# A state-space and SwiGLU block on one core: token blocks of two tiles, and down's weights split once

## The chip, the cores and the metric

The kernel runs on one core of a Trainium2 chip. The core has TensorE for matrix products (PE in the profile, with its weight loads as PEld), VectorE (DVE), ScalarE (ACT) and GpSimd (POOL) for elementwise work, and SyncE (SP), which here issues every DMA. The metric is the device time of one execution in microseconds.

## The reference

The input has 2048 tokens of 448 features. Two residual branches follow each other; both are modulated by six vectors drawn from a condition c.

```
mod = (silu(c) @ w_mod) -> sa, ca, ga, sb, cb, gb
h = layernorm(x) * (1 + ca) + sa
x = x + ga * (causal_conv(h, K) + h * Dskip)      # K from A, B, C, dt, 256 states per feature
h = layernorm(x) * (1 + cb) + sb
x = x + gb * ((silu(h @ w_gate) * (h @ w_up)) @ w_down)   # w_gate, w_up 448 x 1792, w_down 1792 x 448
```

The convolution's kernel K(l) is a sum of exponentials. When its exponents are small over all 2048 steps, the kernel takes K as K(0) plus a slope times l; the convolution is then running sums along the tokens. A test on the chip picks this path (the small path, the one that these inputs take) or a general one.

## The kernel before

The 2048 tokens are 16 tiles of 128 rows; F = 1792 is 14 slices of 128. Tiles are grouped in blocks of 2, 2, 3, 3, 3 and 3 (`BLOCKS`). A block runs the feed-forward branch for its tiles (`ffn`): for each slice f, `gate_up(f)` forms gate and up for all tokens of the block, one matmul of 256 or 384 columns for each pair of weight part and input part, and `down(f - 1)` accumulates the former slice's result for each tile in a PSUM bank (`dn0` to `dn2`). I call gate_up(f) with down(f - 1) a step.

Matmuls use the fast float32r type. To keep float32's precision each operand is split in a high part, rounded by a ScalarE copy, and a low part, the difference; three products of parts replace one. Inputs are split in `transposes` (hhi, hlo), the product silu(gate) * up in `gate_up` (phi, plo, lines 664 to 668), gate's and up's weights in `split_w` (lines 90 to 95), and down's in `split_d` (wdh on ScalarE, line 634; wdl on GpSimd, line 635). Gate's and up's parts are kept on chip after the first block; down's unsplit slices are kept (`wdn`), and split again in every block. In the last block down's weights are first multiplied by gb, on GpSimd.

The first block is special (`fresh`): weights arrive during it. SyncE loads three slices ahead into three staging buffers (`stage`), one slice being four DMAs for gate and up (lines 78 and 79) and one for down (line 84); a staging buffer is free once its slice is split. Before the first block a preamble computes the modulation, K and the first two tiles.

While a block runs, the first branch of the next block's tiles is computed between its steps: `n1` statistics, h (s0), two products with the gates (s1), adding the running sums and splitting (s2), the skip term (s3), three triangular matmuls into `cv` and a bank (s4), and passing the last row on as running sums through a small DMA, line 798 (s5); then `n2` statistics, the normalised tile (`make_xn`), and four groups of transposes between gate_up(13) and down(12), which I call the transition.

The order on every engine is the program's order (`manual_schedule`). The table `TIMES` sets it by hand: its numbers are half steps of a block, h // 2 being the slice after which a stage is put and h % 2 whether before or after down. Tiles in PSUM come from a rotating pool of four banks (`bank`), two for each slice, one for a scan, four for a transition; a bank is given out again when all readers of its former use are done.

```
at(f, late): after gate_up(f), before (late = 0) or after (late = 1) down(f - 1)
at(NF - 1, 0, transposes, nx, new_fl)
```

Of the kernel before, what the change touches and what calls it, by code (L numbers as in the profile page):

```python
# [21 lines left out]
NS = 3  # L22
BLOCKS = [2, 2, 3, 3, 3, 3]
# [3 lines left out]

TIMES = (
# [15 lines left out]
def tile_kernel(ctx, tc, x, a_re, a_im, b_re, b_im, c_re, c_im, log_dt, dskip,  # L44
# [25 lines left out]
    wgu, raw, wdn = {}, {}, {}  # L70
    stage = [const.tile([128, 2, 4, 128], F32, name=f"raw{q}") for q in range(NS)]

# [9 lines left out]
    def load_d(pool, j):  # L82
        wdn[j] = pool.tile([128, D], F32, name=f"wd{j}")
        sy.dma_start(wdn[j], wd[j * 128:(j + 1) * 128, :])

# [13 lines left out]
    tok = const.tile([128, 1], F32)  # L99
    run = const.tile([128, 2, D], F32)  # L100
    ca1 = const.tile([128, D], F32)
# [20 lines left out]
    class Norm:  # L122
# [10 lines left out]
        def root(self, ts):  # L133
            rs = small.tile([128, MB], F32, name="rs" + self.tag)
            n = len(ts)
            po.tensor_scalar(rs[:, 0:n], self.mv[:, 0:n, 1], EPS, None, op0=OP.add)
            po.tensor_tensor(rs[:, 0:n], rs[:, 0:n], mhalf.to_broadcast([128, n]), op=OP.pow)
            for q, i in enumerate(ts):
                self.of[i] = self.mv[:, q, 0:1], rs[:, q:q + 1]
# [8 lines left out]
    def make_h(h, i, part=None):  # L148
        m, rs = n1.of[i]
# [8 lines left out]
    def make_xn(i, new, src=None):  # L158
        src = xs[i] if src is None else src
        xn[i] = new()  # L160
        for o, a, n in ((0, 0, D), (D, 384, 64)):
            ve.tensor_scalar(xn[i][:, o:o + n], src[:, a:a + n], *n2.of[i], op0=OP.subtract, op1=OP.mult)

    def transposes(ts, new):
        n = len(ts) * 128
        for k in range(4):
# [3 lines left out]
            fl = new()  # L170
            sc.activation(hhi[:, k, 0:n], ps[:, 0:n], AF.Identity, scale=cb1c[:, k:k + 1], bias=sbc[:, k:k + 1])
            if k % 2:
                sc.activation(fl[:, 0:n], ps[:, 0:n], AF.Identity, scale=cb1c[:, k:k + 1], bias=sbc[:, k:k + 1])
# [64 lines left out]
    with tc.tile_pool(name="pre", bufs=1) as pre, tc.tile_pool(name="wm", bufs=6) as wm:  # L238
# [166 lines left out]
        for q in range(2):  # L405
            make_xn(q, lambda: pre.tile([128, 512], F32, name="xn", bufs=2), os[q])
# [9 lines left out]
        transposes(TILES[0], lambda: pre.tile([128, MB * 128], F32, name="fl", bufs=2))  # L416
# [6 lines left out]
        for z in range(2):  # L423
            sc.copy(run[0:1, z, :], o[32 * z:32 * z + 1])
# [194 lines left out]
    def run_blocks(pools, st, first=None):  # L619
        work, hid = pools.work, pools.hid  # L620
        new_xn = lambda: work.tile([128, 512], F32, name="xn", bufs=MB)
        new_fl = lambda: hid.tile([128, MB * 128], F32, name="p")
        def ffn(ts, fresh, last, todo):
            n = len(ts) * 128
            dn = [psd.tile([128, 512], F32, name=f"dn{q}") for q in range(len(ts))]
            pp, wp = {}, {}
            qz = [(q, z) for z in range(3) for q in range(len(ts))]

            def split_d(j):
                if last:  # L630
                    po.tensor_tensor(wdn[j], wdn[j], gb, op=OP.mult)
                hi = hid.tile([128, D], F32R, name="wdh")
                lo = hid.tile([128, D], F32R, name="wdl")
                sc.copy(hi, wdn[j])  # L634
                po.tensor_tensor(lo, wdn[j], f32(hi), op=OP.subtract)  # L635
                wp[j] = hi, lo

            def gate_up(f, nw):
                head = fresh and f == 0
                if not head:  # L640
                    split_d(f)
# [22 lines left out]
                ve.tensor_tensor(p[:, 0:n], p[:, 0:n], ps[1][:, 0:n], op=OP.mult)  # L664
                if nw is not None and not head:
                    split_w(nw, 1)
                sc.copy(hi[:, 0:n], p[:, 0:n])  # L667
                ve.tensor_tensor(lo[:, 0:n], p[:, 0:n], f32(hi[:, 0:n]), op=OP.subtract)  # L668
# [30 lines left out]
            for q, i in enumerate(ts):  # L699
                t = dn[q][:, 0:D]  # L700
                if not last:
                    t = new_xn()[:, 0:D]
                    ve.tensor_tensor(t, dn[q][:, 0:D], gb, op=OP.mult)
                ve.tensor_tensor(xs[i], xs[i], t, op=OP.add)
                sy.dma_start(out[i * 128:(i + 1) * 128, :], xs[i])
# [3 lines left out]
        if first is not None:  # L709
# [8 lines left out]
            transposes(TILES[0], new_fl)  # L718
        for b, ts in enumerate(TILES):
            todo = {}  # L720
            if b + 1 < len(TILES):
# [8 lines left out]
                root1, *times, root2, shift = TIMES[min(b, 2)]  # L730
# [4 lines left out]
                for q, (i, hs) in enumerate(zip(nx, times)):  # L735
# [3 lines left out]
                    go(h, n2.stat, i, nx)  # L739
# [4 lines left out]
                at(NF - 1, 0, transposes, nx, new_fl)  # L744
# [4 lines left out]
    def small_path(pools):  # L749
# [3 lines left out]
        def s0(i):  # L753
            h = work.tile([128, D], F32, name="h")
# [5 lines left out]
        def s1(i):  # L760
            h = vs[i]
            v0 = work.tile([128, D], F32, name="v0")
            v1 = work.tile([128, D], F32R, name="v1")
            po.tensor_tensor(v0, h, gm0, op=OP.mult)  # L764
            po.tensor_tensor(v1, h, gm1, op=OP.mult)  # L765
            vs[i] = h, v0, v1

        def s2(i):
            h, v0, v1 = vs[i]
            ve.tensor_tensor(v0[0:1], v0[0:1], run[0:1, 0, :], op=OP.add)  # L770
            po.tensor_tensor(v1[0:1], f32(v1[0:1]), run[0:1, 1, :], op=OP.add)  # L771
# [6 lines left out]
        def s3(i):  # L778
            h = vs[i][0]
            po.tensor_tensor(h, h, gd, op=OP.mult)  # L780
# [10 lines left out]

        def s5(i):
            o, s = vs.pop(i)
            if i + 1 < NT:
                e = slice(96, 128)
                sc.copy(run[e, 1, :], s[e])
# [88 lines left out]
```

## Time and profile before

| | |
|---|---|
| three runs | 515.14, 515.95, 516.49 us, median 515.95 |
| profiled execution | 516.8 us |
| its span, first to last instruction | 514.9 us, mean granted clock 0.982 |
| TensorE busy | 486.1 us, 94%, 2747 matmuls |
| weight loads busy | 454.5 us, 88% |
| VectorE, ScalarE, GpSimd busy | 305.1, 189.0, 226.3 us |
| chain that ended last | TensorE 78%, VectorE 10%, DMA 3% |
| DMA | 26.07 MB, 21.80 MB of them read from HBM |

All times in the views below are microseconds from the start of the span, unless marked ns. A row of the chain or of a timeline has start, duration, engine (SPq is SyncE's queue of DMA issues), source line, operation, destination <- sources, and a count where equal rows are merged; a bracket gives idle time before it and what ended that. A row of the groups has busy time, mean ns of one, and idle time before. Matmuls overlap in the engine's pipeline, so the time of one is read from the start of the next.

The blocks begin at 49.7, 118.4, 180.8, 263.7, 346.6 and 429.5 us, as told by their first gate matmuls; the preamble is what lies ahead of 49.7.

### The profile page before, as it was taken

The numbers are of one execution on the slowest core, as the hardware profiler recorded it, in microseconds if no ns is written. First come the engines' busy times: TensorE is split into PE (matmuls) and PEld (weight loads), VectorE is DVE, ScalarE is ACT, GpSimd is POOL, SyncE is SP. The second block draws the span as 40 slices with busy tenths as digits, with TensorE's granted clock in tenths as the row PEclk, the third lists the DMA queues.
The fourth block names the chain that finished last, engine by engine and source line by source line (L and its number), as shares of the span: only waits on it lengthen the run. The fifth ranks groups of instructions, "written<-read, shape, count | busy, mean of one in ns | idle before, by whom it ended". The sixth has DMA issues, their size and how long they took to land.

```text
span 514.9 us, 7291 instructions
## 1 busy us (share of the span) xinstructions
PE 486.1 (94%) x2747; PEld 454.5 (88%) x2747; DVE 305.1 (59%) x509; ACT 189.0 (37%) x388; POOL 226.3 (44%) x209
## 2 busy tenths in 40 slices
PE   6679979799989999999999999999999999999995
PEld 4345969689879999999999999999999999999995
DVE  1898889987687762675373477275377447211222
ACT  4247735544323432333242333242233324222231
POOL 1468453641765325483212555312446423344330
PEclk8988998999999999999999999999999999999999
DMA  7996555402000020000021000003000001000001
GB/s 209 259 222 174 150 153 158 136 28 90 0 2 2 0 91 0 2 2 0 1 71 37 1 2 1 2 2 107 1 0 2 0 1 53 1 1 0 2 0 61
DMA packets 25860, 26.07 MB, mean 51 GB/s; under 512 B 2232, under 2 KB 25144, under 8 KB 25816
## 3 DMA queue, kind: packets, MB, share of 16 engines
q1 hardware_dynamic: 25816, 25.52, 17.8%
q8 instruction: 23, 0.38, 0.3%
q14 instruction: 21, 0.17, 0.1%
HBM read 21.80 MB, written 3.67 MB: 49 GB/s over the span
## 4 chain that ended last, share of the span: by engine, by line
PE 78%; DVE 10%; DMA 3%; issue 3%; ACT 3%; SPq 2%; POOL 0%; POOLq 0%; DVEq 0%; ACTq 0%
PE bank L653 49%; PE dn L679 23%; PE bank L187 1%; PE bank L169 1%; DVE gu L95 1%; DMA dsk<-in_A_Dskip_dram 1%; DMA raw<-in_B_w_up_dram 1%; DVE scr L334 1%; DVE v L770 1%; DVE h L151 1%; DMA wd<-in_B_w_down_dram 1%; DVE plo L668 1%; SPq L78 1%; DVE t L342 1%; PE cv L786 1%
## 5 line engine op out<-in xcount | busy, mean ns | idle before, releaser
L653 PE MATMUL bank<-hhi,gu 128*128 128x384 f32 (+1 forms) x1169 | 213.4, 322 | 0.4 <-DVE gu L93 0.4
L653 PEld LDWEIGHTS bank<-hhi,gu 128*128 128x128 f32 x1169 | 193.1, 190 | 3.6 <-DVE gu L93 0.6
L635 POOL TENSOR_TENSOR wdl<-wd,wdh 128x448 fp32r<-128x448 f32 x84 | 102.2, 1219 | 203.3 <-ACT wdh L634 191.1
L653 PE MATMUL bank<-hlo,gu 128*128 128x384 f32 (+1 forms) x668 | 132.6, 321 | 0.0
L664 DVE TENSOR_TENSOR p<-p,bank 128x384 f32<-128x384 f32 (+1 forms) x84 | 42.5, 506 | 131.2 <-PE bank L653 127.0
L653 PEld LDWEIGHTS bank<-hlo,gu 128*128 128x128 f32 x668 | 111.0, 190 | 0.0
L667 ACT CAST phi<-p 128x384 fp32r<-128x384 f32 (+1 forms) x84 | 40.1, 477 | 151.0 <-DVE p L664 151.0
L668 DVE TENSOR_TENSOR plo<-p,phi 128x384 fp32r<-128x384 f32 (+1 forms) x84 | 53.8, 641 | 41.0 <-ACT phi L667 41.0
L659 ACT ACTIVATE p<-bank 128x384 f32<-128x384 f32 (+1 forms) x83 | 37.8, 456 | 68.8 <-PE bank L653 68.8
L679 PE MATMUL dn<-wdh,plo 128*128 128x448 f32 x224 | 59.9, 368 | 2.8 <-DVE plo L668 2.6
L679 PE MATMUL dn<-wdh,phi 128*128 128x448 f32 x224 | 60.2, 369 | 1.2 <-ACT phi L667 1.2
L679 PE MATMUL dn<-wdl,phi 128*128 128x448 f32 x224 | 59.5, 366 | 0.8 <-POOL wdl L635 0.8
L634 ACT CAST wdh<-wd 128x448 fp32r<-128x448 f32 x84 | 47.6, 567 | 31.7 <-PE dn L679 31.6
L679 PEld LDWEIGHTS dn<-wdh,plo 128*128 128x128 f32 x224 | 41.8, 188 | 7.5 <-DVE plo L668 4.3
L679 PEld LDWEIGHTS dn<-wdl,phi 128*128 128x128 f32 x224 | 42.0, 188 | 4.6 <-POOL wdl L635 1.1
L679 PEld LDWEIGHTS dn<-wdh,phi 128*128 128x128 f32 x224 | 39.8, 188 | 3.1 <-ACT phi L667 1.6
L764 POOL TENSOR_TENSOR v<-h,gm 128x448 f32<-128x448 f32 x14 | 16.2, 1154 | 14.2 <-DVE h L153 14.2
L774 ACT CAST vh<-v 128x448 fp32r<-128x448 f32 x14 | 7.9, 566 | 33.1 <-DVE v L770 33.1
L187 PE MATMUL bank<-wmt,cs 112*128 112x448 f32 (+1 forms) x32 | 15.4, 632 | 4.8 <-DMA wmt<-in_w_mod_dram 4.8
L765 POOL TENSOR_TENSOR v<-h,g 128x448 fp32r<-128x448 f32 x14 | 18.5, 1319 | 0.0
L771 POOL TENSOR_TENSOR v<-v,run 1x448 fp32r<-1x448 f32 x14 | 17.0, 1212 | 2.5 <-DMA run<-run 1.5
L187 PEld LDWEIGHTS bank<-wmt,cs 112*128 112x128 f32 (+1 forms) x32 | 6.2, 205 | 12.6 <-issue 9.6
(167 smaller groups left out, 447.1 us busy)
## 6 DMA issues: line engine op xcount, KB each, us to landing
wmt<-in_w_mod_dram SPq DMA_DIRECT2D x6, 784.0 KB
x<-in_A_u_dram SPq DMA_DIRECT2D x16, 224.0 KB
out_dram<-x SPq DMA_DIRECT2D x16, 224.0 KB
wd<-in_B_w_down_dram SPq DMA_DIRECT2D x14, 224.0 KB
raw<-in_B_w_gate_dram SPq DMA_DIRECT2D x14, 192.0 KB
raw<-in_B_w_up_dram SPq DMA_DIRECT2D x14, 192.0 KB
raw<-in_B_w_gate_dram SPq DMA_DIRECT2D x14, 64.0 KB
raw<-in_B_w_up_dram SPq DMA_DIRECT2D x14, 64.0 KB
```

The source lines that it names most:

```text
L187: pe.matmul(ps[0:rows, 0:D], cs[:, k:k + 1].to_broadcast([P, rows]), w[k], start=k == 0, stop=k == 3)
L634: sc.copy(hi, wdn[j])
L635: po.tensor_tensor(lo, wdn[j], f32(hi), op=OP.subtract)
L653: pe.matmul(ps[s][:, 0:n], w[:, s, a], (hlo if lo else hhi)[:, k, 0:n], start=not lo and a == 0, stop=lo and k == 3)
L659: sc.activation(p[:, 0:n], ps[0][:, 0:n], AF.Silu)
L664: ve.tensor_tensor(p[:, 0:n], p[:, 0:n], ps[1][:, 0:n], op=OP.mult)
L667: sc.copy(hi[:, 0:n], p[:, 0:n])
L668: ve.tensor_tensor(lo[:, 0:n], p[:, 0:n], f32(hi[:, 0:n]), op=OP.subtract)
L679: pe.matmul(dn[q][:, 0:D], u[:, cs], v, start=f == 0 and z == 0, stop=f == NF - 1 and z == 2)
L764: po.tensor_tensor(v0, h, gm0, op=OP.mult)
L765: po.tensor_tensor(v1, h, gm1, op=OP.mult)
L771: po.tensor_tensor(v1[0:1], f32(v1[0:1]), run[0:1, 1, :], op=OP.add)
```

## The change

- Blocks are eight of two tiles. The x tiles on chip are four instead of six, as are other buffers that go by the block's size, and `TIMES` has new half steps.
- Down's slices arrive in three staging buffers of their own (`stage_d`). Their parts are made once, in the first block, and kept for all blocks; the low part is made by VectorE. SyncE loads down's slice f + 3 behind gate's and up's slice f + 5, where before both parts of slice f + 5 came together.
- In the first block, the branch of the next tiles takes the products with the gates and the skip term on VectorE, and the triangular matmuls of the first product in full float32, with the running sums added by one-row matmuls (s14); nothing is split there.
- The product silu * up and the transposed inputs are written back to their PSUM banks instead of SBUF, and split from there.
- `make_xn` runs on ScalarE, with a bias that GpSimd makes (two small operations in `root`), save for the very first tile.
- gb is multiplied on VectorE at the end of every block; the very last tile is finished and stored in two halves.

```diff
-BLOCKS = [2, 2, 3, 3, 3, 3]
+BLOCKS = [2] * 8
 TIMES = (
-    (3, (6, 8, 8, 9, 11, 11), (12, 14, 15, 17, 20, 20), 21, (24, 25)),
-    (3, (6, 8, 9, 10, 10, 11), (10, 10, 13, 13, 15, 16), (15, 16, 18, 18, 21, 21), 22, (24, 24, 24)),
-    (3, (7, 8, 8, 10, 10, 10), (10, 13, 13, 14, 14, 15), (14, 17, 17, 18, 18, 19), 20, (24, 24, 24)),
+    (3, (4, 6, 9, 10, 12), (7, 8, 16, 17, 18), 19, (20, 21)),
+    (3, (4, 5, 9, 11, 12, 13, 14), (6, 8, 16, 17, 18, 19, 20), 21, (22, 23)),
 )
...
+    stage_d = [const.tile([128, D], F32, name=f"rawd{q}") for q in range(NS)]
...
     def load_d(pool, j):
-        wdn[j] = pool.tile([128, D], F32, name=f"wd{j}")
+        wdn[j] = stage_d[j % NS]
+        wp[j] = [pool.tile([128, D], F32R, name=f"wd{q}{j}") for q in "hl"]
         sy.dma_start(wdn[j], wd[j * 128:(j + 1) * 128, :])
+
+    def split_d(j):
+        hi, lo = wp[j]
+        sc.copy(hi, wdn[j])
+        ve.tensor_tensor(lo, wdn[j], f32(hi), op=OP.subtract)
...
+            if self is n2:
+                po.tensor_tensor(ng[:, 0:n], self.mv[:, 0:n, 0], rs[:, 0:n], op=OP.mult)
+                po.tensor_scalar(ng[:, 0:n], ng[:, 0:n], -1.0, None, op0=OP.mult)
...
-            ve.tensor_scalar(xn[i][:, o:o + n], src[:, a:a + n], *n2.of[i], op0=OP.subtract, op1=OP.mult)
+            if on_v:
+                ve.tensor_scalar(xn[i][:, o:o + n], src[:, a:a + n], m, rs, op0=OP.subtract, op1=OP.mult)
+            else:
+                sc.activation(xn[i][:, o:o + n], src[:, a:a + n], AF.Identity, scale=rs, bias=ng)
...
-                ve.tensor_scalar(fl[:, 0:n], ps[:, 0:n], cb1c[:, k:k + 1], sbc[:, k:k + 1], op0=OP.mult, op1=OP.add)
-            ve.tensor_tensor(hlo[:, k, 0:n], fl[:, 0:n], f32(hhi[:, k, 0:n]), op=OP.subtract)
+                ve.tensor_scalar(ps[:, 0:n], ps[:, 0:n], cb1c[:, k:k + 1], sbc[:, k:k + 1], op0=OP.mult, op1=OP.add)
+            ve.tensor_tensor(hlo[:, k, 0:n], ps[:, 0:n], f32(hhi[:, k, 0:n]), op=OP.subtract)
...
-            def split_d(j):
-                if last:
-                    po.tensor_tensor(wdn[j], wdn[j], gb, op=OP.mult)
-                hi = hid.tile([128, D], F32R, name="wdh")
-                lo = hid.tile([128, D], F32R, name="wdl")
-                sc.copy(hi, wdn[j])
-                po.tensor_tensor(lo, wdn[j], f32(hi), op=OP.subtract)
-                wp[j] = hi, lo
...
-                if not head:
+                if fresh and not head:
                     split_d(f)
...
-                ve.tensor_tensor(p[:, 0:n], p[:, 0:n], ps[1][:, 0:n], op=OP.mult)
+                ve.tensor_tensor(ps[1][:, 0:n], p[:, 0:n], ps[1][:, 0:n], op=OP.mult)
...
-                sc.copy(hi[:, 0:n], p[:, 0:n])
-                ve.tensor_tensor(lo[:, 0:n], p[:, 0:n], f32(hi[:, 0:n]), op=OP.subtract)
+                sc.copy(hi[:, 0:n], ps[1][:, 0:n])
+                ve.tensor_tensor(lo[:, 0:n], ps[1][:, 0:n], f32(hi[:, 0:n]), op=OP.subtract)
...
-                    pools.load(f + 2 + NS)
+                    pools.load(f + 2 + NS, f + NS)
...
-                t = dn[q][:, 0:D]
-                if not last:
-                    t = new_xn()[:, 0:D]
-                    ve.tensor_tensor(t, dn[q][:, 0:D], gb, op=OP.mult)
-                ve.tensor_tensor(xs[i], xs[i], t, op=OP.add)
-                sy.dma_start(out[i * 128:(i + 1) * 128, :], xs[i])
+                t = new_xn()[:, 0:D]
+
+                h = D // 2 if last and q == len(ts) - 1 else D
+                for a in range(0, D, h):
+                    c_ = slice(a, a + h)
+                    ve.tensor_tensor(t[:, c_], dn[q][:, c_], gb[:, c_], op=OP.mult)
+                    ve.tensor_tensor(xs[i][:, c_], xs[i][:, c_], t[:, c_], op=OP.add)
+                    sy.dma_start(out[i * 128:(i + 1) * 128, c_], xs[i][:, c_])
...
+        def s14(i):
+            h, v0, v1 = vs[i]
+            o = psd.tile([128, 512], F32, name="cv")[:, 0:D]
+            s = bank()[:, 0:D]
+            pe.matmul(o, f32(tri), v0, start=True, stop=False)
+            pe.matmul(s, tri, v1, start=True, stop=False)
+            pe.matmul(s, f32(tri[0:1, :]), run1[0:1], start=False, stop=True)
+            pe.matmul(o, f32(tri[0:1, :]), run0[0:1], start=False, stop=True)
+            s3(i, True)
+            ve.tensor_tensor(xs[i], h, xs[i], op=OP.add)
+            vs[i] = o, s
...
+        return lambda fresh: (s0, lambda i: s1(i, True), s14, s5) if fresh else (s0, s1, s2, s3, s4, s5)
```

More of the change, by code (lines that the diff above doesn't have):

```diff
@@ L415, in tile_kernel @@
             split_w(0, z)
-        transposes(TILES[0], lambda: pre.tile([128, MB * 128], F32, name="fl", bufs=2))
+        transposes(TILES[0])
         o = psd.tile([128, 512], F32, name="cv")[:, 0:D]
@@ L422, in tile_kernel @@
         sc.copy(xs[1], os[1])
-        for z in range(2):
-            sc.copy(run[0:1, z, :], o[32 * z:32 * z + 1])
+        sc.copy(run0[0:1], o[0:1])
+        sc.copy(run1[0:1], o[32:33])
         po.tensor_scalar(hd[0], gm1, tok, None, op0=OP.mult)
@@ L753, in s0, with s1 @@
         def s0(i):
-            h = work.tile([128, D], F32, name="h")
+            h = work.tile([128, D], F32, name="h", bufs=2)
             make_h(h, i)
             vs[i] = h
-        def s1(i):
+        def s1(i, on_v=False):
             h = vs[i]
[L762 to L765, printed above, removed]
+            v0 = work.tile([128, D], F32, name="v0", bufs=2)
+            v1 = work.tile([128, D], F32R, name="v1", bufs=2)
+            for v, g in ((v0, gm0), (v1, gm1)):
+                (ve if on_v else po).tensor_tensor(v, h, g, op=OP.mult)
             vs[i] = h, v0, v1
@@ L795, in s5 @@
                 e = slice(96, 128)
[L796 to L797 removed]
+                sc.copy(run1[e], s[e])
+                ve.scalar_tensor_tensor(run0[e], run1[e], 128.0, o[e], op0=OP.mult, op1=OP.add)
                 sy.dma_start(run[0:1], run[127:128])
```

55 lines of the change are left out of this document (28 added, 27 removed).

## The prediction

> **What bounds the kernel now.** I read the page's busy shares first (TensorE busy 94% of the span), then a table of stages: the first block of two tiles, the second, and the third, the first of three tiles. Columns after the length are busy time and instruction count of TensorE, its weight loads, VectorE, ScalarE and GpSimd, then granted clock, DMA share and GB/s.
>
> ```profile
> 49.70:118.40 68.70, 61.07 (x411) 56.11 (x410) 60.64 (x90) 37.39 (x83) 34.10 (x28) 0.98 0.43 123
> 118.40:180.80 62.40, 60.09 (x416) 56.38 (x415) 47.55 (x80) 24.06 (x55) 32.37 (x30) 0.97 0.06 19
> 180.80:263.70 82.90, 82.90 (x457) 80.84 (x457) 46.51 (x83) 28.83 (x56) 33.70 (x30) 1.00 0.05 15
> ```
>
> The third block has TensorE busy for all of 82.90 us: matmuls alone set it, and 34 us of GpSimd beside it cost nothing. Slack to win lies only in the first two blocks. Next the chain of waits, for the pace of a step (gate and up for one slice of F, then down for the slice before): two tiles in the second block, three in the third.
>
> ```profile
> 124.85 2.61 PE bank L653 x22
> ...
> 128.69 2.62 PE bank L653 x22
> ...
> 188.53 1.82 PE dn L679 x9
> ...
> 194.23 1.82 PE dn L679 x9
> ```
>
> A step takes 3.84 us with two tiles (1.92 a tile) and 5.70 with three (1.90 a tile). In the second block 14 x 3.84 = 53.8, 1.3 of transposes and three scans of 0.6 (three matmuls of 448 columns at 0.203, a twelfth of the 2.44 us of L679 quoted below) make 56.9 of 62.4 us: 5.5 us of stall. In the first block, 14 steps, one transition (1.0), two scans and the small extras make about 57 of 68.7: some 12 us of stall.
>
> Then what the first block waits for: SyncE's DMA issues, the chain at one of them, and ScalarE's split of a weight slice.
>
> ```profile
> 62.68 0.38 SPq L78 DMA_DIRECT2D raw<-in_B_w_gate_dram  x1
> ...
> 87.08 0.64 SPq L798 DMA_DIRECT2D run<-run  x1
> ...
> 90.17 1.66 SPq L84 DMA_DIRECT2D wd<-in_B_w_down_dram  x1
> ```
> ```profile
> 90.17 3.98 DMA wd<-in_B_w_down_dram
> ```
> ```profile
> 66.01 0.41 ACT L91 CAST gu<-raw 128x256 fp32r<-128x256 f32 x1 [0.81 <-DMA raw<-in_B_w_up_dram]
> ```
>
> SyncE issues five sets (gate, up and down of one slice) without a gap in 24.4 us, 4.88 us a set, slower than TensorE's 3.84; ScalarE's wait shows a late landing. A down slice lands 3.98 us after its issue began, 2.3 after it ended. VectorE is the other limit (60.64 of 68.7 busy):
>
> ```profile
> 73.30 1.25 DVE L95 TENSOR_TENSOR gu<-raw,gu 64x256 fp32r<-64x256 f32 x1
> ...
> 102.58 0.42 DVE L664 TENSOR_TENSOR p<-p,bank 128x256 f32<-128x256 f32 x1
> 102.92 0.95 DVE L93 TENSOR_TENSOR gu<-raw,gu 128x768 fp32r<-128x768 f32 x1
> 103.79 0.42 DVE L668 TENSOR_TENSOR plo<-p,phi 128x256 fp32r<-128x256 f32 x1
> 104.24 0.42 DVE L95 TENSOR_TENSOR gu<-raw,gu 64x256 fp32r<-64x256 f32 x1
> 104.69 0.62 DVE L789 TENSOR_TENSOR x<-h,x 128x448 f32<-128x448 f32 x1
> ```
>
> The same operation (L95) takes 0.42 us or 1.25: the long ones stand beside a GpSimd operation on two SBUF tensors.
>
> **The change, part by part.**
>
> *Down's split once.* It removes 70 of the 84 GpSimd subtractions of this row, and as many ScalarE copies (mean 1219 and 567 ns):
>
> ```profile
> L635 POOL TENSOR_TENSOR wdl<-wd,wdh 128x448 fp32r<-128x448 f32 x84 | 102.2, 1219 | 203.3 <-ACT wdh L634 191.1
> ...
> L634 ACT CAST wdh<-wd 128x448 fp32r<-128x448 f32 x84 | 47.6, 567 | 31.7 <-PE dn L679 31.6
> ```
>
> In the later blocks that is worth nothing: TensorE covers it (third stage row). In the first block 14 subtractions move to VectorE, 14 x 0.62 = 8.7 us more there (the price of the 128x448 row L789), and GpSimd falls nearly silent, which takes the long forms away. VectorE's step is then 0.42 + 0.95 + 0.42 + 0.42 + 0.62 = 2.83; the work of two tiles (about a dozen operations of 0.62 each, gates and skip now among them, splits and scan inputs gone) adds some 15. That is 2.83 x 14 + 15, about 55 us: it fits, but steps that carry tile work come to 5.4.
>
> *Loads in the first block.* Down's slices move behind gate and up of a slice two later in SyncE's queue, through three staging tiles, each freed by a split three steps earlier, so those waits are met early. All sets stay needed, so the pace stays 4.88. From 62.68, eight sets (gate and up of 6 to 13, down of 4 to 11) end at 101.7; two moves of the running sums (0.64 each) and two more slices of down (1.66 each) end at 106.3; the last lands 2.3 later, 108.6. Behind it come ScalarE's copy 0.57 and SiLU 0.4 (as a 256-column copy, 0.41 at L667 below), product 0.42, copy 0.41, subtraction 0.42 with gaps of some 0.1 each: 111.2. The fourth pair of transposes (0.26) and two downs (2.44) follow: the second block starts at 113.9 rather than 118.4: -4.5. Bounds: TensorE alone (next item) 111.0, so -7.4; no gain, 0.
>
> *The branch in float32.* These matmuls run two records each:
>
> ```profile
> 14.11 1.67 PE L320 MATMUL dn<-x,ident 128*128 128x448 f32 x4
> ```
>
> Two take 1.67 us with a pipeline's end; I take 0.75 each. Three of them and one fast one (0.20) make 2.45 a tile against 0.61, so +3.7 for two tiles. TensorE's own sum for the first block: 49.7 + 53.8 + 4.9 + 0.7 (the gate's broadcast, one more float32 matmul) + 1.9 (transition, below) = 111.0. Loads end later, so this is covered; if loads keep up it is the bound. It saves VectorE's and ScalarE's splits and one wait on the running sums.
>
> *Head.* The second tile's normalisation moves to ScalarE, behind the copy of the first tile; the head may start later by that copy and its own, up to 0.9 (two short of 0.57). Step 1 already waited for VectorE:
>
> ```profile
> 52.96 0.97 PE L653 MATMUL bank<-hhi,gu 128*128 128x256 f32 x6 [0.39 <-DVE gu L93]
> ```
>
> So I take 0; cover gone, +0.5.
>
> *Blocks of two.* Twelve tiles go from 1.90 to 1.92 us a tile-step: 168 x 0.02 = +3.4. Per matmul a 256-column one takes 2.61/22 = 0.119 us. The Trainium skill, page "TensorE: Matmul & The Clock Gate", section "Back-to-back issue gap", gives columns/2.4 ns plus 2.5: an estimate of 0.109 and, for 384 columns, 0.163, by which this term would be +1.6; the rows have more per matmul, and they decide. The second block's stall goes (-5.5): its table squeezed three tiles' scan into 54 us beside GpSimd's subtractions; the new one has two, each stage one to four steps behind its input, and GpSimd free. If it stayed, +5.5.
>
> *Transitions.* Six in the later blocks instead of four, and longer. Product and its two parts now pass through PSUM in place, so a bank lives until the low part is taken, not until the product. Four transposes take the banks of the last two slices; the fourth takes the newest. The chain, then weight loads, VectorE, ScalarE at the first transition, and the chain at a three-tile one:
>
> ```profile
> 114.95 1.02 PE bank L169 x8
> 115.98 2.44 PE dn L679 x12
> ...
> 258.72 1.31 PE bank L169 x12
> ```
> ```profile
> 115.53 0.20 PEld L169 LDWEIGHTS bank<-ident,xn 128*128 128x128 f32 x2 [0.16 <-DVE p L664]
> ```
> ```profile
> 115.06 0.42 DVE L664 TENSOR_TENSOR p<-p,bank 128x256 f32<-128x256 f32 x1 [0.53 <-PE bank L169]
> 115.95 0.42 DVE L668 TENSOR_TENSOR plo<-p,phi 128x256 fp32r<-128x256 f32 x1 [0.47 <-ACT phi L667]
> ```
> ```profile
> 115.52 0.41 ACT L667 CAST phi<-p 128x256 fp32r<-128x256 f32 x1 [1.39 <-DVE p L664]
> ```
>
> Already now the fourth pair waits 0.16 for the product, done at 115.48. After the change it waits for the low part, done at 116.37: 0.89 more, with everything behind it on TensorE. A transition costs 1.02 + 0.89 = 1.9: six make 11.4 against four of 1.31, 5.2: +6.2. Bounds: 0.9 if the wait were hidden, +7 if PSUM writes were slower.
>
> *x loads.* Four x tiles instead of six: a load waits for an output's store; the store starts about 1.3 us into the block, store and load take up to 3.98 each (the landing above), so it lands nine in, and the low part that waits behind it on VectorE is needed at about thirteen. Nothing; cover gone, a microsecond a block.
>
> *Tail.*
>
> ```profile
> 508.05 1.84 DVE L704 TENSOR_TENSOR x<-x,dn 128x448 f32<-128x448 f32 x3 [0.66 <-PE dn L679]
> ...
> 508.86 0.37 PE L679 MATMUL dn<-wdh,plo 128*128 128x448 f32 x1
> ```
>
> TensorE ends at 509.2, the last add at 509.9. After: a whole tile's product and add from 0.6 before TensorE's end (1.3 us), then two halves of 0.8 each: 1.7 us later than now. Less queues before the last store, which is half as long; I take +0.9, between +0.4 and +1.7.
>
> **Sum:** -4.5 + 3.4 - 5.5 + 6.2 + 0.9 = +0.5 us. The profiled execution took 516.8 (span 514.9), 0.85 above the median of the runs, 515.95; so 517.3 for such an execution and 516.5 for the median.
>
> **Rivals.**
>
> *Loads keep up.* TensorE sets the first block: 111.0 instead of 113.9, -2.9: 513.6. For: one of the five sets' pace may come from ScalarE and VectorE freeing stages late; against: 24.4 us without a gap. The Trainium skill, page "DMA: Bandwidth & Descriptors", section "Specifications", has 512 B pieces at line rate and about 358 GB/s of HBM per core; by that estimate a set would take under 2 us. This case's 123 GB/s over the stage speaks against it. Chance 0.15.
>
> *The fourth bank's wait is hidden.* Then 7 x 0.89 = 6.2 fewer: 510.3. For: 0.16 is small; against: the low part's end is a fixed 1.3 us behind the gate's. Chance 0.10.
>
> *VectorE holds the first block (slower side).* With 8.7 us more, its steps of 5.4 delay each staging tile's release, then the next load. From 115.0 for the second block's start the kernel is over 0.3% slower; with no gain, 118.4, it takes 521.0. For: 60.64 of 68.7 busy now; against: 55 counted. Chance 0.25.
>
> *A stall in every later block* as in today's second: each microsecond is six, at 1.5 us 525. Against: the new table's distances. Chance 0.08.
>
> **How the numbers follow.** The forecast, trades that cancel, has 0.42, own range 514 to 519. 0.3% is 1.5 us, about what a measurement tells from no change: of the forecast 0.29 lies within, 0.09 slower, 0.04 faster. Faster: 0.04 + 0.13 + 0.10 = 0.27; slower: 0.09 + 0.25 + 0.08 = 0.42; same 0.31. The range 511 to 521.5 leaves out the hidden wait's lower half and the stalls.
>
> **What would show it.** The second block's start (113.9); SyncE's issues gapless at 4.9 us a set; in each transition weight loads of the transposes waiting about 1.0 us for the low part; a step at 3.84 in all later blocks with TensorE idle nowhere else; the last add 2.3 us behind TensorE's end. The forecast is wrong if the first block ends outside 112 to 116, or if ScalarE or VectorE wait inside a later block for a running sum or an x load.

## The result, and the profile after

The changed kernel takes 519.40 us (median of 5 runs, 518.83 to 520.80) against 515.95 (5 runs, 515.14 to 517.30): a ratio of 1.008 with a 95% interval of 1.0057 to 1.0102, slower by 3.5 us, where the forecast had +0.5. The profiled executions' spans are 517.6 and 514.9 us. The table of stages of the kernel after, with the columns of the prediction's first fence: the first block, the second, the last.

```profile
49.81:113.94 64.13, 62.58 (x419) 57.20 (x418) 52.41 (x101) 36.82 (x84) 3.36 (x6) 0.98 0.44 128
113.94:171.04 57.10, 56.31 (x409) 54.68 (x408) 30.84 (x63) 17.25 (x42) 11.73 (x14) 1.00 0.06 17
...
456.54:510.75 54.21, 54.21 (x393) 52.29 (x391) 14.77 (x33) 10.59 (x28) 0.00 (x0) 1.00 0.03 10
```

The second block's start is at 113.94, as forecast (113.9), and VectorE's first block is 52.4 us instead of 60.6. Blocks two to seven take 57.10 us each, to 0.01 us. Next the chain of waits with a step and two block starts, and the weight loads at the first transition:

```profile
113.94 5.27 PE bank L659 x44
...
120.43 2.64 PE bank L659 x22
...
124.29 2.64 PE bank L659 x22
...
171.04 5.27 PE bank L659 x44
```
```profile
111.06 0.20 PEld L186 LDWEIGHTS bank<-ident,xn 128*128 128x128 f32 x2 [1.03 <-DVE plo L674]
```

A step is 3.86 us. In a block, 57.10 less a transition (1.87) and two scans (1.23) leaves 3.857 for each of 14 steps, where the forecast had 3.84. The weight loads of the transposes wait 1.03 us for the low part; the table of waits (who waited, for whom, us in total, times, longest) adds this up to 7.2 us in seven transitions.

The first block's chain, and SyncE's and VectorE's rows that belong to it, look different from the forecast:

```profile
84.04 0.46 PE bank L659 x4
84.50 3.85 DMA run<-run
88.35 0.04 issue
88.39 1.01 PE bank L809 x2
89.41 0.75 PE cv L810 x2
```
```profile
78.30 0.63 DVE L820 SCALAR_TENSOR_TENSOR run<-run,cv 32x448 f32<-32x448 f32 x1
```
```profile
60.48 0.38 SPq L79 DMA_DIRECT2D raw<-in_B_w_gate_dram  x1
...
82.81 1.59 SPq L86 DMA_DIRECT2D rawd<-in_B_w_down_dram  x1
84.50 0.65 SPq L821 DMA_DIRECT2D run<-run  x1
...
94.19 0.38 SPq L79 DMA_DIRECT2D raw<-in_B_w_gate_dram  x1
...
98.89 0.60 SPq L821 DMA_DIRECT2D run<-run  x1
99.59 0.99 SPq L86 DMA_DIRECT2D rawd<-in_B_w_down_dram  x2
```

The sets are gapless at 4.82 us (seven from 60.48 to 94.19, one move among them), as forecast. But the last down slices are issued by 100.6, 5.7 us ahead of the forecast, and hold nothing at the end. What TensorE waits for, ahead of the transition, is the move of the running sums: ready on VectorE at 78.93, issued at 84.50 because the loads stand ahead of it, landed at 88.35. The tail, VectorE's first and last operation:

```profile
510.16 0.62 DVE L711 TENSOR_TENSOR xn<-dn,gb 128x448 f32<-128x448 f32 x1 [0.72 <-PE dn L685]
...
512.51 0.39 DVE L712 TENSOR_TENSOR x<-x,xn 128x224 f32<-128x224 f32 x1
```

TensorE ends at 510.75, the last add 2.15 us behind it, the span 6.85 behind it (5.67 before).

| term | forecast | measured in the two profiles |
|---|---|---|
| second block's start | -4.5 | -4.5 (118.41 to 113.94) |
| steps of two tiles | +3.4 | +5.2 (98 of 3.857 for 14 of 3.84 and 56 of 5.696) |
| second block's stall | -5.5 | -5.5 |
| transitions | +6.2 | +6.0 (six of 1.87, four of 1.31) |
| tail | +0.9 | +1.2 |
| sum | +0.5 | +2.4; the spans differ by 2.7 |

### The profile page after: what moved, and what is told of

Its sections match the earlier page's. It is cut to its first block, busy times and chain, and to the rows that moved or that the text cites. A ratio compares the mean times of both kernels' runs of the same rounds, so it can differ in the third digit from the quotient of the medians.

```text
span 517.6 us, 8533 instructions
## 1 busy us (share of the span) xinstructions
PE 493.8 (95%) x3371; PEld 461.8 (89%) x3371; DVE 286.1 (55%) x568; ACT 174.3 (34%) x414; POOL 102.0 (20%) x127
## 4 chain that ended last, share of the span: by engine, by line
PE 90%; DVE 4%; DMA 2%; ACT 2%; issue 1%; SPq 0%; DVEq 0%
PE bank L659 56%; PE dn L685 26%; PE bank L203 2%; DMA dsk<-in_A_Dskip_dram 1%; PE dn L406 1%; PE bank L186 1%; DVE scr L350 1%; PE bank L236 1%; DMA run<-run 1%; DVE bank L670 1%; DVE plo L674 1%; DVE h L164 1%; ACT phi L673 1%; PE bank L796 0%; PE cv L797 0%
## 5 line engine op out<-in xcount | busy, mean ns | idle before, releaser
L659 PE MATMUL bank<-hhi,gu 128*128 128x256 f32 x1561 | 223.9, 283 | 0.0
L659 PEld LDWEIGHTS bank<-hhi,gu 128*128 128x128 f32 x1561 | 210.1, 191 | 4.2 <-ACT phi L673 0.7
L659 PE MATMUL bank<-hlo,gu 128*128 128x256 f32 x892 | 143.4, 283 | 0.0
L670 DVE TENSOR_TENSOR bank<-p,bank 128x256 f32<-128x256 f32 x112 | 47.9, 428 | 142.8 <-PE bank L659 141.7
L659 PEld LDWEIGHTS bank<-hlo,gu 128*128 128x128 f32 x892 | 123.1, 192 | 0.0
L673 ACT CAST phi<-bank 128x256 fp32r<-128x256 f32 x112 | 41.7, 372 | 144.8 <-DVE bank L670 144.8
L665 ACT ACTIVATE p<-bank 128x256 f32<-128x256 f32 x111 | 42.4, 382 | 129.2 <-PE bank L659 128.9
L674 DVE TENSOR_TENSOR plo<-bank,phi 128x256 fp32r<-128x256 f32 x112 | 47.4, 423 | 44.3 <-ACT phi L673 44.3
L780 POOL TENSOR_TENSOR v<-v,run 1x448 fp32r<-1x448 f32 x12 | 13.8, 1146 | 49.6 <-DMA run<-run 49.6
L187 ACT ACTIVATE hhi<-bank,sbc,cb1c 128x256 fp32r<-128x256 f32 x32 | 16.5, 575 | 0.3 <-PE bank L186 0.3
L789 POOL TENSOR_TENSOR h<-h,gd 128x448 f32<-128x448 f32 x12 | 16.4, 1365 | 0.0
```

Source lines behind the costliest of these rows:

```text
L659: pe.matmul(ps[s][:, 0:n], w[:, s, a], (hlo if lo else hhi)[:, k, 0:n], start=not lo and a == 0, stop=lo and k == 3)
L665: sc.activation(p[:, 0:n], ps[0][:, 0:n], AF.Silu)
L670: ve.tensor_tensor(ps[1][:, 0:n], p[:, 0:n], ps[1][:, 0:n], op=OP.mult)
L673: sc.copy(hi[:, 0:n], ps[1][:, 0:n])
L674: ve.tensor_tensor(lo[:, 0:n], ps[1][:, 0:n], f32(hi[:, 0:n]), op=OP.subtract)
L780: po.tensor_tensor(v1[0:1], f32(v1[0:1]), run1[0:1], op=OP.add)
```

## The experiments

Each ratio is to the kernel before, run on the same chip beside it. Where two profiles are compared, blocks two to eight repeat to 0.05 us, but the first block does not, so it is told apart from them.

**Product in SBUF.**

```diff
-                ve.tensor_tensor(ps[1][:, 0:n], p[:, 0:n], ps[1][:, 0:n], op=OP.mult)
+                ve.tensor_tensor(p[:, 0:n], p[:, 0:n], ps[1][:, 0:n], op=OP.mult)
...
-                sc.copy(hi[:, 0:n], ps[1][:, 0:n])
-                ve.tensor_tensor(lo[:, 0:n], ps[1][:, 0:n], f32(hi[:, 0:n]), op=OP.subtract)
+                sc.copy(hi[:, 0:n], p[:, 0:n])
+                ve.tensor_tensor(lo[:, 0:n], p[:, 0:n], f32(hi[:, 0:n]), op=OP.subtract)
```

> The product silu * up goes back to an SBUF tile, and its parts are taken from there; all else as after. Forecast's theory: in each of seven transitions the fourth pair of transposes waits 1.03 us for the low part, because the product's bank lives until then. Free at the product instead, 0.87 earlier: each transition goes from 1.87 to about 1.0, 7 x 0.87 = 6.1 us less, 513.3. If writing the product to PSUM is also what makes a step 3.854 us instead of 3.840, 98 x 0.014 = 1.4 more goes: 511.9. Rival (the wait only stands in for the next one, the inputs' parts on VectorE and ScalarE): less than 2 us, 517.5 or more.

514.71 us, ratio 0.9975 (0.9944 to 1.0007). The table of waits, then two block starts of the chain:

```profile
PEld bank L186 <- DVE p L670: 1.2, 7, 0.2
```
```profile
172.19 5.28 PE bank L659 x44
...
228.46 5.27 PE bank L659 x44
```

A block takes 56.27: 0.83 less, and the wait that remains is 0.17 in each of seven. The wait theory holds. The extra 1.4 us does not appear: steps are still 2.63 + 1.22 us, so writing the product to PSUM is not what lengthens them.

**Five banks.**

```diff
-    psg = ctx.enter_context(tc.tile_pool(name="psg", bufs=4, space=PS))
+    psg = ctx.enter_context(tc.tile_pool(name="psg", bufs=5, space=PS))
...
-                ps = [psd.tile([128, 512], F32, name="dn2") if head else bank(), bank()]
+                ps = [bank(), bank()]
```

(end_gate and one tile of the preamble take a rotating bank likewise.)

> A fifth rotating PSUM bank (the bank that only the head and the preamble used); the product stays in PSUM in place. The fourth pair of transposes then takes the silu's bank of the newest slice, free some 2 us earlier. Wait theory: 6.1 us less as with the product in SBUF, 513.3. The step stays at 3.854 if PSUM in place is what lengthens it, and what this kernel and the one with the product in SBUF differ by is the price of that (1.4 us, or nothing). Rival (the next wait takes over): less than 2 us.

513.70 us, ratio 0.9969 (0.9940 to 0.9999).

```profile
167.87 5.27 PE bank L659 x44
...
223.96 5.27 PE bank L659 x44
```

A block takes 56.09, 1.01 less than after; no transpose waits any more. The two kernels differ by the 0.17 of wait that the SBUF product leaves, and by nothing else in these blocks. So the transitions' wait is a matter of which bank comes free. Seven times 0.83 or 1.01 is 5.8 or 7.1 us in the whole kernel (the ratios of the three kernels differ by 5.4 and 5.7 us), and either remedy takes it away.

**The move on GpSimd's queue.**

```diff
-                sy.dma_start(run[0:1], run[127:128])
+                (po if i < 4 else sy).dma_start(run[0:1], run[127:128])
```

> The two moves of the running sums in the first block are issued on GpSimd's queue instead of SyncE's, where the first stood ready at 78.93 us and was issued at 84.50 behind the loads. Theory (a move behind loads, not the loads themselves, is what the first block waited for): the move lands before 83.5, the wait of 1.31 us on it goes and the second block starts 1 to 2 us earlier, at 112 to 113: 517.5 to 518.4. Rival of the prediction (the loads' pace sets the end): the second block starts at 113.9 again, 519.4. Rival (GpSimd's own issue is slow): the move lands later than 88.35 and the block ends later.

519.70 us, ratio 1.0081 (1.0055 to 1.0108). GpSimd's row, and two of the three TensorE rows of the first block with idle time ahead of them (the third is the transition's):

```profile
78.56 0.75 POOL L821 DMA_DIRECT2D run<-run  x1 [16.98 <-DVE run L820]
```
```profile
84.56 1.10 PE L659 MATMUL bank<-hhi,gu 128*128 128x256 f32 x7 [0.54 <-ACT p L665]
105.28 0.67 PE L685 MATMUL dn<-wdh,phi 128*128 128x448 f32 x2 [0.65 <-ACT phi L673]
```

The wait on the move is gone, as the theory says, but the second block starts at 113.72, not 112 to 113, and the time is that of the change: two waits on ScalarE, 0.54 and 0.65 us, took its place. In the first, ScalarE's copy of a down slice had waited 2.65 us for its landing (83.6), and the operations behind it in its order were late. In the second, ScalarE had waited for GpSimd's bias for the normalised tiles; the chain goes back from there over VectorE to another landing of down (91.5). The gain went into the next wait, so the theory of the move alone falls; loads stand behind both waits.

**Less of down loaded.**

```diff
-        sy.dma_start(wdn[j], wd[j * 128:(j + 1) * 128, :])
+        w = D if j < NP0 else 64
+        sy.dma_start(wdn[j][:, 0:w], wd[j * 128:(j + 1) * 128, 0:w])
```

> From the fourth slice on, only 64 of down's 448 columns are loaded (the rest of a staging tile keeps old values, so the output is wrong); the instructions, their order and all waits are those of after. A slice's bytes go from 736 to 544 KB. Theory (bytes are the pace of the first block: sets of 4.7 to 4.9 us whatever queue issues them): sets shrink to about 3.6 us, below TensorE's step, the running sums' move is not late, and the first block takes TensorE's own 62 to 62.7 us, less than in any of eight executions so far (63.4 to 69.4). Rival (ScalarE and VectorE, not the bytes, hold staging back): sets stay at 4.7 to 4.9 and the block at 63.4 to 69.4.

516.90 us, ratio 1.0039 (1.0017 to 1.0061): some 2 us of the change's 1.008 are gone, with intervals that just overlap. The stage and the chain at the second scan:

```profile
48.35:111.29 62.94, 62.15 (x419) 56.85 (x418) 52.68 (x103) 37.65 (x85) 3.89 (x7) 0.99 0.35 99
```
```profile
85.61 0.20 PE bank L809
85.82 0.94 PE bank L810 x2
86.76 0.75 PE cv L811 x2
```

TensorE waits neither for the move nor for ScalarE: the first block is 62.94 us, shorter than in any other execution, and that is TensorE's own; it idles only in the transition. The sets are another matter: six take 4.28 us each (64.91 to 90.61), not 3.6, and SyncE still issues them with gaps of less than 0.5 us, so the transfers remain the loads' pace and are merely quick enough now. A quarter fewer bytes made a set only a tenth shorter, so its bytes alone are not its price. The five kernels with the change's own transition and weight loads have first blocks of 64.3 to 69.4 us, so waits for loads, with the lower clock described in the last section, cost 1.4 to 6.4, by execution.

**Down's loads on a second queue**, on top of five banks.

```diff
-        sy.dma_start(wdn[j], wd[j * 128:(j + 1) * 128, :])
+        (po if NP0 <= j else sy).dma_start(wdn[j], wd[j * 128:(j + 1) * 128, :])
```

> Five rotating banks as in bank5, and in the first block down's slices are loaded from GpSimd's queue instead of SyncE's. Later blocks 56.1 us as there. First block: SyncE's set goes from 4.85 us to about 3.3 (four issues without the 1.6 of down's), and the running sums' move is no longer queued behind it. Theory (the issues of one queue are the pace of the first block): it shortens from 63.4 to 67.4 us (four executions) to TensorE's own 62 (54 of steps, 0.75 of gate, two scans of 2.65, a transition of 1.0, and 1 at the start). Rival (the bytes are the pace, 155 GB/s with these pieces): nothing changes, 63.4 to 67.4 again. Rival (GpSimd's issue is slow): longer.

515.31 us, ratio 1.0007 (0.9973 to 1.0040). A set on SyncE's queue, now without down:

```profile
71.49 2.13 SPq L79 DMA_DIRECT2D raw<-in_B_w_gate_dram  x1
73.73 0.53 SPq L80 DMA_DIRECT2D raw<-in_B_w_gate_dram  x1
74.31 1.33 SPq L79 DMA_DIRECT2D raw<-in_B_w_up_dram  x1
75.70 0.57 SPq L80 DMA_DIRECT2D raw<-in_B_w_up_dram  x1
76.36 1.91 SPq L79 DMA_DIRECT2D raw<-in_B_w_gate_dram  x1
```

A set takes 4.87 us with four issues as with five: they stretch (0.4 to 2.1 us for the first of them). The first block, 66.98 us, is no shorter, so the theory of the issues falls. The transfers are the pace, 736 KB in 4.8 us or about 155 GB/s, not the queue that issues them. What in a transfer takes the time stays open: the profile has the 16 DMA engines busy 0.55 of it.

**Four staging buffers.**

```diff
-NS = 3
+NS = 4
...
-                p = hid.tile([128, MB * 128], F32, name="p")
+                p = hid.tile([128, MB * 128], F32, name="p", bufs=1)
...
-                    pools.load(f + 2 + NS, f + NS)
+                    pools.load(f + 2 + NS, f + 3)
```

> Four staging buffers for gate's and up's slices instead of three, each loaded one slice earlier (silu's tile has one buffer to make room); down's three, the order of loads else, and the bytes are those of after. Theory (the DMA engines set the pace of 4.8 us a set, so a deeper queue changes nothing): sets of 4.7 to 4.9 us, the second block's start in the spread so far, 111.8 to 116.2. Rival (the loop through three buffers is the pace: landing 5.4 to 5.8 us, ScalarE's copies 2.3, issue 1.9 make about 9.6 us for two sets): sets become shorter until TensorE stops waiting, and the second block starts near 111.3 as with less of down loaded.

525.96 us, ratio 1.0167 (1.0127 to 1.0207): neither expectation. Before the next down slice SyncE issues two sets of gate and up alone:

```profile
54.25 1.47 SPq L79 DMA_DIRECT2D raw<-in_B_w_gate_dram  x1
...
58.47 1.38 SPq L79 DMA_DIRECT2D raw<-in_B_w_gate_dram  x1
...
62.49 1.62 SPq L86 DMA_DIRECT2D rawd<-in_B_w_down_dram  x1
```

They take 4.22 and 4.02 us for 512 KB, nearly as much as the 736 KB of a whole set, and about what a set with little of down takes. So most of a set's price lies with gate's and up's transfers, whose rows are 128 floats where down's are 448; no run changes that length, so that it is the cause is not shown. Whole sets then average 4.85 us (64.21 to 93.31): a fourth buffer for gate and up does not quicken them, though down keeps three and TensorE's clock halves in this stretch, so the loop through the buffers is not excluded for good. But the second block starts at 121.03. TensorE's timeline and the clock (the last but two column) say why:

```profile
70.14 1.12 PE L685 MATMUL dn<-wdh,phi 128*128 128x448 f32 x2 [2.91 <-ACT phi L673]
72.55 1.70 PE L807 MATMUL cv<-v,tri 128*128 128x448 f32 x2
```
```profile
66.00:70.00 4.00, 1.23 (x11) 1.03 (x9) 1.42 (x3) 2.06 (x5) 0.00 (x0) 0.93 0.46 124
70.00:74.00 4.00, 3.86 (x9) 2.82 (x9) 3.90 (x8) 1.38 (x4) 0.00 (x0) 0.50 0.55 166
74.00:78.00 4.00, 4.00 (x7) 1.34 (x6) 3.94 (x8) 1.32 (x4) 0.00 (x0) 0.50 0.62 179
```

Gate's and up's deeper queue puts down's slice later, TensorE idles 2.9 us for it, and then runs at half its clock for some 12 us, which costs about 6 us, twice the idle time. The first block takes 71.6 us.

**Down's parts made anew in every block**, on ScalarE and GpSimd.

```diff
-                if fresh and not head:
+                if not head:
                     split_d(f)
...
-        ve.tensor_tensor(lo, wdn[j], f32(hi), op=OP.subtract)
+                po.tensor_tensor(lo, wdn[j], f32(hi), op=OP.subtract)
```

> Down's slices are split anew in every block, high part on ScalarE and low part on GpSimd, as before the change; blocks of two, table and all else as after. Theory of the prediction (worth nothing in later blocks, since TensorE covers 14 x 1.2 us on GpSimd in 57): blocks of 57.1 as in after, and the stall of the second block was the table's. Rival (GpSimd's subtractions made the stall): blocks grow by the stall of the old second block, up to 5.5 us in each of six, up to 33 us in all. In the first block GpSimd makes 14 subtractions beside VectorE's splits again: its length tells what moving them to VectorE was worth, 0 to 4 us.

520.02 us, ratio 1.0098 (1.0070 to 1.0125). One block's group row, and two block starts:

```profile
L641 POOL TENSOR_TENSOR wdl<-wd,wdh 128x448 fp32r<-128x448 f32 x14 | 16.5, 1182 | 20.3 <-ACT wdh L640 20.3
```
```profile
169.71 5.28 PE bank L659 x44
226.81 5.28 PE bank L659 x44
```

57.10 us a block with 16.5 us more on GpSimd: keeping the parts is worth nothing there. The first block (64.69) lies among the others too, so moving its low parts to VectorE won nothing that this can show.

**Blocks of three again, with the rest of the change** and the product in SBUF (the old table from the second block on; to make room, h and its products have one buffer, the parts of a product share the normalised tile's buffers, and the second tile's h comes later in the first block).

```diff
-BLOCKS = [2] * 8
+BLOCKS = [2, 2, 3, 3, 3, 3]
```

> Blocks of 2, 2, 3, 3, 3, 3 again, with the rest of the change: down's parts kept, the first block's branch in float32 on TensorE with its splits on VectorE, and the product in SBUF. The second block computes three tiles' branch in 54 us by the old table. Theory: what pays in the change is the first block and GpSimd's silence in the second; two-tile blocks only cost. First gate at 49.6, then blocks of 64.3, 57.5 (54 of steps, three scans of 0.6, a transition of 1.3 and almost no stall, since GpSimd has about 15 us of work there instead of 32), 82.9 three times, 79.8 and a tail of 6.9: a span of 506.8, 508.6 us. Rival (the table's squeeze of three tiles' scans, not GpSimd, made the second block's stall): that block keeps 62.4 us, 513.5.

507.85 us, ratio 0.9865 (0.9827 to 0.9904): faster than both kernels.

```profile
112.73 5.27 PE bank L660 x44
...
131.14 1.58 DVE v L780
132.72 0.02 issue
132.74 0.58 ACT xn L784
...
171.19 7.67 PE bank L660 x44
```

The second block takes 58.46 us against 62.38 before: with the old table and GpSimd quiet, 4 of the 5.5 us of stall go. With the new table and GpSimd busy (the former experiment) all of it went. So most of the stall needed both, three tiles in the old table and GpSimd's subtractions. GpSimd's part is not isolated here: the normalised tiles are made on ScalarE too, and buffers differ. Against the product in SBUF, from which this kernel differs by the grouping and those buffers, TensorE takes 6.2 us less from the second block's start to its end (385.6 for 391.8), although some stall is left in its second block: blocks of two cost at least that.

**The tail**, first without the last block's gate and halves, then with the last tile whole.

```diff
+                if last:
+                    ve.tensor_tensor(xs[i], xs[i], dn[q][:, 0:D], op=OP.add)
+                    sy.dma_start(out[i * 128:(i + 1) * 128, :], xs[i])
+                    continue
```

> The last block's product with gb is left out and its two tiles are added and stored whole, as the kernel before does it with scaled weights; so the last two tiles' output lacks the gate. It prices the tail: TensorE's end to the last instruction was 5.67 us before and 6.85 after. Theory (VectorE's two more operations and two halves): 1.2 us less, 518.2, with the last add about 0.7 behind TensorE's end instead of 2.15. Rival (the store of a whole tile takes back what VectorE saves): within 0.4 us, 519.0 to 519.4.

518.84 us, ratio 1.0051 (1.0026 to 1.0076). TensorE's end to the span's end is 5.31 us against 6.81 to 7.17 in eight executions with the change's tail: 1.5 to 1.9 for the gate and the halves, more than the theory's 1.2, and the store takes nothing back. The last add is 0.66 behind TensorE's end, for 0.7 expected.

```diff
-                h = D // 2 if last and q == len(ts) - 1 else D
+                h = D
```

> The very last tile is finished and stored whole, not in two halves. VectorE has two operations of 0.62 us instead of four of 0.38: its end moves from 2.15 us behind TensorE's to about 1.9, and the store is twice as long. If the half store was worth what the prediction thought, the tail is 7.1 to 7.6 us instead of 6.85 to 7.1; if the store's cost is its fixed latency, 6.6 to 6.9.

One execution, 521.11 us; its tail is 6.35 us, 0.5 to 0.8 shorter than with halves. VectorE has 0.26 of it. Behind the last add whole stores take 4.46 to 5.01 us (this one, the one without the gate, and both profiles of the kernel before) and half ones 4.66 to 5.01, so halving wins nothing there. Its first block, 69.35 us, is the longest of the five with the change's own transition and weight loads:

```profile
89.06 1.01 PE L809 MATMUL bank<-run,tri 1*128 1x448 f32 x2 [1.51 <-DMA run<-run]
```
```profile
90.00:94.00 4.00, 4.00 (x14) 3.09 (x13) 3.83 (x8) 1.75 (x5) 0.00 (x0) 0.60 0.63 180
```

The same wait on the move, 0.76 us in the first profile of the change, is 1.51 here, and the clock falls to 0.60 behind it.

**The faster kernel with the whole tail and more distance in the second block.**

```diff
-    (3, (6, 8, 9, 10, 10, 11), (10, 10, 13, 13, 15, 16), (15, 16, 18, 18, 21, 21), 22, (24, 24, 24)),
+    (3, (5, 6, 8, 9, 11, 11), (11, 11, 14, 14, 16, 16), (16, 17, 18, 18, 21, 21), 22, (24, 24, 24)),
```

> Blocks of 2, 2, 3, 3, 3, 3 with the product in SBUF (best3), the last tile stored whole, and in the second block's table one and a half steps between a tile's sums and its matmuls where there was a half. Theory: the second block loses the 1.4 us of stall that best3 has there (58.5 to 57.1), the tail goes from about 7.0 to 6.4: 2 us less than best3's 507.85, 505.9. Rival (the stall moves to the next tile's sums, the tail is a draw): within 0.7 of best3.

509.00 us, ratio 0.9887 (0.9860 to 0.9914): a miss. Its second block takes 59.21 us, not 57.1. The first tile's scan no longer waits, the other two wait longer. The tail is 7.13 against 7.88; in sum no difference beyond the intervals.

**The kernel before, once more.**

> The kernel before, once more under the profiler, for its first block alone. If bytes are the pace of the first block in both kernels, the second block's start is a draw here too; if the change took something off it, it lies 2 to 5 us behind the 111.8 to 116.2 of the eight executions with the change, near the 118.4 of the first profile. Rival (the first profile was an unlucky draw and the change won nothing there): 112 to 116.

The kernel is unchanged; one execution, 513.91 us. Its second block starts at 115.62 instead of 118.41, since its first gate is at 46.0 instead of 49.7; the first block is 69.6 against 68.7. Later blocks agree to 0.01 us. The stall with the clock behind it:

```profile
73.85 0.47 PE L786 MATMUL cv<-vh,tri 128*128 128x448 f32 x1 [2.67 <-ACT vh L774]
```
```profile
74.00:78.00 4.00, 4.00 (x18) 3.60 (x19) 3.51 (x6) 3.28 (x9) 2.05 (x2) 0.57 0.51 145
```

The starts of the second block in five executions with the change's own transition and weight loads (the change and four of its variants) are 112.6, 113.7, 113.9, 116.0 and 116.2, in two of the kernel before 115.6 and 118.4: a gain of 2.5 us by the means, and neither end is fixed to better than 2 us. By the block's own length it is 2.9 (66.2 against 69.2). The new start lies where the rival put it, 112 to 116, so that the change shortened the first block is likely, and not shown.

## Why the prediction was right, and where it was not

The forecast, trades that cancel to about nothing, named every term that moved. The median came out 2.9 us above it, inside the range of 511 to 521.5 but just outside the forecast's own, 514 to 519; and the kernel is 0.8% slower, clear of noise, where the forecast itself had no change that one can tell. The larger chance, 0.42, stood on slower, mostly for reasons that did not come: VectorE holding the first block, a stall in every block. By its own steps:

- **Down's split once**: nothing in later blocks, shown by the parts made anew. VectorE was counted at 55 us in the first block and has 52.4. The rival in which VectorE holds that block is out: TensorE waits for VectorE there only in the transition (0.79 us), and with the 14 subtractions taken off VectorE the block is not shorter.
- **Loads in the first block**: right in the number, wrong in the way. The step that failed is "the last lands 2.3 later, 108.6": the eight sets began 2.2 us earlier than I started them (60.48 for 62.68), and the two last slices took 1.0 us together, not 3.3. TensorE's own sum was the nearer bound (61.3 forecast, 62.94 measured), and on top of it came a wait that I had not costed: the move of the running sums, which I counted in SyncE's queue (its row at 87.08 stands in the fence) but not as something that TensorE waits for behind the loads. That it gave 113.9 is luck of one draw; 112.6 to 116.2 is what executions give.
- **Loads keep up** (rival): not so. By the Trainium skill, page "DMA: Bandwidth & Descriptors", section "Specifications", a set would take about 2.1 us, an estimate from 736 KB at its 358 GB/s (the prediction wrote under 2). No run shows it; the sets took 4.8 whatever queue issued them. The rival's number is right where the loads are lighter: with less of down the second block starts at 111.29 for its 111.0.
- **The branch in float32**: 2.64 us a tile against 2.45 forecast; one of the three float32 products takes 0.94 in place of 0.75. Called covered by loads; it is a part of TensorE's sum, which is the floor of the block.
- **Head**: forecast nothing, and nothing shows: first gates at 46.8 to 49.6 in five executions with the change, 46.0 and 49.7 before.
- **Blocks of two**: the term that was mis-sized most, +5.2 for +3.4. A step of the old two-tile block (3.84) was taken over, and the new kernel's is 3.857. It is so in every kernel here with the change, product in PSUM or not, parts kept or not; the cause is open. The estimate from the Trainium skill, page "TensorE: Matmul & The Clock Gate", section "Back-to-back issue gap" (+1.6), was further off; that section calls its formula the gap of a single matmul by itself, not of a stream.
- **The second block's stall**: gone, -5.5 as forecast. Of the two reasons named, either alone takes away most or all of it.
- **Transitions**: 1.87 for 1.9, with the wait at 1.03 for about 1.0, and two experiments that take it away and get 0.83 and 1.01 a block. Of the rivals, the hidden wait is out.
- **x loads**: nothing to TensorE, which idles in the later blocks only in the transitions. But the prediction's own sign of being wrong, a wait of ScalarE or VectorE on a load or a running sum there, did come, small: VectorE waits twice, 0.2 us each, for an x tile. GpSimd waits for the move of the running sums in six blocks, 49.6 us in all, at no cost.
- **Tail**: +1.2 in the profile, +1.1 to +1.5 over the executions, for +0.9; the last add at 2.15 for 2.3. What was wrong is the half store, taken as a help: it costs VectorE 0.26 and wins nothing behind it.
- **Time from the profile**: 0.85 us was taken off, since the profile of before stood that much above its median. The profile of after stands on its median (519.4), so 0.85 of the miss is this draw, about 2 are the steps and the tail.

## What to carry to other kernels

Cost a wider change term by term, and look for the terms that only the grouping causes: here the blocks of two brought 5.2 us of steps and 0.9 of transitions (six of 1.02 for four of 1.31), and the product in PSUM 5.1 more in those six. Together they ate all of what the other parts won. With blocks of three again and the product in SBUF, the kernel is 1.3% under the one before. A buffer that now lives through one more operation (the product in PSUM) is paid wherever the next user comes right behind, once per block. And a small transfer that an engine waits for should not stand in a queue behind bulk loads; but before crediting its removal, ask which wait is next.

## What the runs showed that was not expected

- After a TensorE stall of 1.45 to 2.9 us the granted clock fell to between 0.50 and 0.85 for 4 to 12 us in most cases (before: 2.66 us, then 0.85 and 0.72, and again in its second block: 1.45, then 0.74 and 0.83; with the whole tail: 1.51, then 0.60; with four staging buffers: 2.91, then 0.50), and not after 0.76 or 0.85. It is not a fixed threshold: 1.45 in the first block of the kernel before and 1.51 in the kernel with blocks of three had none, 0.66 with the parts made anew had 0.81 and 0.76. The Trainium skill, page "TensorE: Matmul & The Clock Gate", section "What's actually happening", tells of a clock gate that watches activity in a free-running window of about 3.4 us, so that the moment matters. Two stalls of 1.45 us in one run, one with and one without the fall, fit that; but stalls well under that length were enough.
- The first block's length varies by 5 us between executions of nearly the same program (64.3 to 69.4), later blocks by 0.05. Part of it is that clock, which is low at the start of some blocks too: 0.71 over the first 4 us of the change's, where gate and up of the first slice took 6.29 us, for 5.27 in the run with down's loads on a second queue. Another part may be that a later first gate meets more of the loads done (first gate at 46.80 and a block of 69.35, at 49.61 and 64.33); a gate at 47.92 with a block of 64.69 does not fit, and it is not shown.
- Steps of three tiles became shorter in the faster kernel (its third block 82.58 us against 82.89) while those of two became longer than in the kernel before (3.857 for 3.84). No run here says why.
